# A decode kernel of two layers of cached attention and MLP on one core: w2 loaded by 14 rows a partition, wo in four transfers, softmax maxima and sums through TensorE, and a new order of the instructions

## The chip, the cores and the metric

The kernel runs on one core of a Trainium2 chip. The metric is the device time of one launch in microseconds (us). The engines are TensorE (PE, with its weight load PEld), VectorE (DVE), ScalarE (ACT), GpSimd (POOL) and SyncE (SP), which here only issues DMAs. Every engine works through its own list in order and waits on semaphores for the others.

## What is computed

Two equal layers: layernorm, attention over the last 1,024 positions of a cache of 4,096, residual; layernorm, MLP with silu, residual. Both layers use the same caches and the same weights. There are 8 rows (the batch, one new token each), D = 448, 16 query heads on 8 kv heads of 256, F = 1,792; all bf16.

```python
def attention(x):                       # x: 8 x 448
    q = (x @ wq) -> 16 heads of 256
    k = k_cache[:, :, 3072:4096, :]     # 8 rows x 8 kv heads x 1024 x 256; v likewise
    scores = q . k * 256 ** -0.5        # two query heads share a kv head
    o = softmax(scores) . v
    return o @ wo                       # 4096 x 448

def mlp(x):
    return silu(x @ w1) @ w2            # 448 x 1792, 1792 x 448

x = x + attention(layernorm(x)); x = x + mlp(layernorm(x))
x = x + attention(layernorm(x)); x = x + mlp(layernorm(x))
```

## The kernel before

**What is read.** The window of each row and kv head is one k and one v tile of 128 partitions x 2,048 elements (512 KB). The 128 tiles, 64 MB, are read once. They go through 30 slots of SBUF: the n-th load goes to slot n modulo 30 and waits until load n - 30 is used up. The order on SP's queue is: x, parts of wq and w1, the rest of wq (L444), the k tiles of row 0 (L500), then w2 in four transfers (L459), wo in one (L453), the v tiles of row 0, w1, the k tiles of row 1, its v tiles, and so on. w2 goes to 32 partitions with each transfer: partition 32j + p takes pairs of rows of the j-th quarter. wo goes to 128 partitions with one transfer. Both arrive in pieces of two rows, 1,792 bytes, since each pair of rows has places for the negative row means beside it. These means come from row sums: four groups of w2 and eight of wo, by turns on DVE (`tensor_reduce`, L479) and ACT (448 columns each with an accumulator, L487). Every row sum of wo waits for the whole of wo. The products with w2 (L762) and wo (L721) wait for the means.

**What is done with a tile, and in which order.** Both layers use a tile while it is in its slot. Layer 1 of row b + 1 and layer 2 of row b are woven together; between the layers of a row lies what the code calls its chain. Below, "0" or "1" behind a step's name is layer 1 or layer 2.

1. DVE transposes each k tile in place, in two halves (L636, 16 a row). PE forms the scores for four kv heads at a time (32 matmuls, L651), two lots for each layer, into a bank with head and position on the partitions.
2. Softmax: DVE takes the negative maximum of each partition (max, L663). Four partitions q hold the parts of one head, so DVE transposes (mT, L665), reduces over four (mg, L666) and transposes back (mb, L668). ACT takes the exponential (L671), PE permutes (perm, L673), DVE transposes 32 x 32 blocks (turn, L675). The sum of a head comes from a product with ones (l, L677), a reduction on DVE (lsum, L679) and a reciprocal (rl, L681).
3. PE multiplies with the v tiles, kv head by kv head (PV, 4 matmuls each, L687). ACT evicts the bank of 512 columns (oev, L694), PE transposes (oT, 4 matmuls, L696), and DVE evicts with the factor 1/l (oTev, L700). Layer 1 does this for heads 0 to 6 and then for head 7 alone, with a second eviction of the whole bank. PE multiplies with wo (32 matmuls, L721), ACT evicts (rowb, L727), and the fold (seven matmuls, L531 and L534) brings the row onto the partitions, added to x, with the mean in a column of its own.
4. The chain: DVE subtracts the mean and masks half columns (xb, L732). PE computes w1 (16 matmuls, L541), then the sum of squares (stat, four matmuls, L739). ACT scales it (var, L742), POOL takes the power -1/2 (L744). DVE transposes w1's result (w1T, L546), ACT takes tanh (L756), DVE finishes silu (hT, L757). PE multiplies with w2 (14 matmuls, L762) and folds; xb and stat follow again, x2b keeps the row on ACT (L768), then wq in two lots (L773), each with a transpose (qT, L778), a scaling by 1/sigma (qm, L779) on DVE, four matmuls (qx, L786) and an eviction on ACT (L790), which layer 2's scores wait for.
5. wo and the MLP of layer 2 are done for rows 0 to 6 together (`final_rows`, w1 and w2 through L541 and L856) while the last row's scores run, and for row 7 alone at the end (`final_last`).

The last chunk of 448 = 3 x 128 + 64 rows of w1 and wq lies in two halves of 64 partitions, one for either half of the columns. The mask sets the other half of the column vector to zero, and the matmuls read all 128 partitions.

**What sets the order.** The code does not write down a sequence. Each step is a task with an engine, keys that it reads and writes, and an estimated duration (`pe(...)`, `dve(...)`, `act(...)`, `pool(...)`, `dma(...)`). The class `Plan` gives each task a rank, the longest chain of estimated durations behind it. A list scheduler then gives each engine, when it comes free, the ready task of highest urgency, which is the rank plus an entry of the table `BIAS`, empty here. What comes out is fixed in the program: a list for each engine, with the semaphore waits. On the chip nothing is reordered.

Of the kernel before, what the change touches and what calls it, by code (L numbers as in the profile page):

```python
# [4 lines left out]
BF16 = mybir.dt.bfloat16  # L5
# [15 lines left out]
BIAS = {}  # L21
# [14 lines left out]
class Plan:  # L36
# [9 lines left out]
    def add(self, eng, fns, reads=(), writes=(), dur=0.1, row=-1, name="", dma_key=None, via="sp"):  # L46
        if not isinstance(fns, (list, tuple)):
            fns = [fns]
        t = Task(eng, list(fns), dur, row, name)
# [202 lines left out]
def bass_interleave_layers__sliding_block_cached__dense_activation_silu__decode_kernel(  # L252
# [43 lines left out]
    th = sb("th", [P, FC], F32)  # L296
    hT = sb("hT", [P, FC], BF16)
    q1s = sb("q1s", [P, NB, P], BF16)
    mm = [sb(f"mm{i}", [P, 32], F32) for i in range(2)]
    mg = [sb(f"mg{i}", [P, 8], F32) for i in range(2)]  # L300
    xb0 = sb("xb0", [P, XC + 1, NB], BF16)
    xl0 = sb("xl0", [P, NB], BF16)
    cols = sb("cols", [P, 10], BF16)
    fcols = sb("fcols", [P, 16], F32)
# [3 lines left out]
    e_sb = [qbd[i][:, 264:520] for i in range(2)]  # L308
    oT2 = [q1s[:, b, 0:2 * H] for b in range(NB)]
    x2b = [q1s[:, b, 32:32 + XC + 1] for b in range(NB)]  # L310
    oT1 = [q1s[:, b, 40:40 + 2 * H] for b in range(NB)]
    rl = [q1s[:, b, 72:72 + 2 * H].bitcast(F32) for b in range(NB)]
# [4 lines left out]
    eps4, nhalf, var4, rhalf = fcols[:, 9:10], fcols[:, 10:11], fcols[:, 11:12], fcols[:, 12:13]  # L317
    ones_b = ones_1.broadcast_to([P, P])
# [7 lines left out]
    C_O, C_ST = 128, 200  # L326
# [31 lines left out]
    SCRATCH = {R - 1: ["xrow", "xh", "sq8", "sqh8", "st8", "q1T", "sel", "sel_f", "nm8", "rh8"] +  # L358
# [10 lines left out]
    sel_f = SCR[:, 1152:1152 + 4 * H].bitcast(F32)  # L369
    big8 = SCR2[:, 0:512].bitcast(F32)  # L370
# [13 lines left out]
    const(cols[:, :], 0.0, ["cols0"])  # L384
    const(ones_1, 1.0, ["ones_1"], ["cols0"])
    for q in range(4):
# [3 lines left out]
    for i in range(2):  # L390
        const(mm[i][:], 0.0, [("mm", i)])
        const(mg[i][:], 0.0, [("mg", i)])
    const(qbd[0][:, 0:8], 0.0, [("pad", 0)])
    const(qbd[1][:], 0.0, [("pad", 1)] + QB(1, 0) + QB(1, 1), dur=0.2)
    for i in SC:
        const(bank[i][:], -1e30, bk(i), dur=0.6)
# [19 lines left out]
    for q in range(4):  # L416
# [6 lines left out]
    dve(lambda e: e.tensor_copy(sel_o[:], sel_f.rearrange("p (n a) -> p a n", a=2)), ["sel_f"], ["sel_o"], 0.1, -1,  # L423
        "init")
# [27 lines left out]
    def load_wo():  # L452
        dma(lambda e: e.dma_start(wo_sb[:].rearrange("p (h n) -> p h n", n=PW)[:, :, R0:M1],  # L453
                                  A_wo.rearrange("(h p a) n -> p h (a n)", p=P, a=2)), ["wo"], HD * D * 2, "wo",
            rate=375e3)

    def load_w2():
        for j in range(4):
# [290 lines left out]
    def up(b):  # L749
        w1_rows(XB, 1, lambda c: xbt[b][:, c:c + 1], b, [("xbt", b)], "w1")  # L750
# [274 lines left out]
```

## Time and profile before

| | us |
|---|---|
| runs without profile | 255.55, 252.28, 256.36 (median 255.55) |
| the profiled execution | 251.9 |
| its span, first to last instruction | 249.6 |
| PE busy (3,055 matmuls) | 165.3 |
| DVE busy (432) | 166.2 |
| ACT busy (151) | 60.1 |
| k transposes on DVE (L636), 128 | 83.3 |
| scores on PE (L651), 1,024 matmuls | 41.0 |
| products with v on PE (L687), 512 matmuls | 37.3 |
| maxima (L663), 16 of 0.424 | 6.8 |
| 77.3 MB on queue q1 | 82.6% of 16 DMA engines' span |

How to read it: in the profile's slices, each of 40 equal parts of the span has a digit, the busy share in tenths; `PEclk` is the clock that TensorE was granted, in tenths of full speed (mean 0.942 here), DMA the mean busy share of the 16 DMA engines, and GB/s what they moved. A chain of waits is followed back from the last instruction; each line gives start, length and what the time went to. "SPq" is SP's queue, where a DMA instruction waits until its slot is free. In a table by stages, each engine has its busy us and the number of its instructions in brackets.

### The profile page before, as it was taken

To read this page: it belongs to the slowest core of one execution; us is meant where nothing else is said; L and a number is where in the kernel's file an instruction comes from. 1 tells how busy PE (TensorE), PEld (TensorE's weight loads), DVE (VectorE), ACT (ScalarE), POOL (GpSimd) and SP (SyncE) were. 2 spreads that over 40 slices of the span, in tenths; PEclk is the share of its full clock that TensorE was granted. 3 is DMA by queue.
4 is the path that set the end of the run, shared out by engine and by line. 5 is a ranking of instruction groups with operands and counts; after the bars stand their busy time and mean duration, and the time that the engine had idled before them with its cause. 6 is when DMAs were issued, how large, how long until landed. Compare 5 with 4: busy or idle time off the path is not lost.

```text
span 249.6 us, 7017 instructions
## 1 busy us (share of the span) xinstructions
PE 165.3 (66%) x3055; PEld 85.2 (34%) x3055; DVE 166.2 (67%) x432; ACT 60.1 (24%) x151; POOL 23.0 (9%) x41
## 2 busy tenths in 40 slices
PE   0054211257687976878787787878788967888783
PEld 0053100012243334334334533443434434434532
DVE  6749536794885797599587768946783697534321
ACT  2000033721213221331331222232111331323221
POOL 1201000000000010100010010000000000001200
PEclk9999999999589999999997999999657999999995
DMA  6999999999999999999999899999967997300000
GB/s 173 416 407 351 200 278 387 409 413 418 407 362 301 412 410 362 389 412 403 315 411 409 322 376 413 410 343 412 407 257 259 418 392 294 158 3 4 3 1 3
DMA packets 22676, 78.13 MB, mean 313 GB/s; under 512 B 2279, under 2 KB 5366, under 8 KB 22262
## 3 DMA queue, kind: packets, MB, share of 16 engines
q1 hardware_dynamic: 22486, 77.31, 82.6%
q8 instruction: 24, 0.39, 0.6%
q10 hardware_dynamic: 160, 0.38, 0.5%
q14 instruction: 6, 0.05, 0.1%
HBM read 77.67 MB, written 0.01 MB: 311 GB/s over the span
## 4 chain that ended last, share of the span: by engine, by line
PE 34%; DMA 25%; DVE 21%; SPq 8%; ACT 5%; issue 4%; POOL 2%; DVEq 0%; ACTq 0%
DMA slot<-in_A_k_cache_dram 14%; DVE slot L636 11%; PE bank L651 11%; DMA wo_sb<-in_A_wo_dram 11%; PE bank L687 4%; DVE slot L479 3%; PE bank L773 3%; SPq L459 3%; SPq L500 3%; PE bank L541 3%; PE bank L721 3%; PE bank L786 2%; PE bank L762 2%; ACT qbd L790 2%; POOL fcols L744 2%
## 5 line engine op out<-in xcount | busy, mean ns | idle before, releaser
L636 DVE STREAM_TRANSPOSE slot<-slot 128x512 uint32<-128x512 uint32 x128 | 83.3, 686 | 15.3 <-DMA slot<-in_A_k_cache_dram 15.0
L651 PE MATMUL bank<-slot,qbd 128*16 128x256 bf16 (+1 forms) x1024 | 41.0, 305 | 15.1 <-ACT qbd L790 6.4
L687 PE MATMUL bank<-slot,qbd 128*8 128x512 bf16 (+7 forms) x512 | 37.3, 393 | 15.2 <-DMA slot<-in_A_v_cache_dram 9.2
L651 PEld LDWEIGHTS bank<-slot,qbd 128*16 128x16 bf16 (+1 forms) x1024 | 27.8, 94 | 23.5 <-ACT qbd L790 8.4
L687 PEld LDWEIGHTS bank<-slot,qbd 128*8 128x8 bf16 (+7 forms) x512 | 12.4, 89 | 29.7 <-DMA slot<-in_A_v_cache_dram 12.9
L773 PE MATMUL bank<-wq_sb,q1s 128*1 128x512 bf16 x256 | 19.9, 434 | 1.9 <-DVE q1s L732 1.9
L694 ACT ACTIVATE ot<-bank 128x512 bf16<-128x512 f32 x24 | 14.3, 597 | 26.6 <-PE bank L687 26.6
L721 PE MATMUL bank<-wo_sb,q1s 128*1 128x449 bf16 x288 | 19.1, 378 | 1.1 <-DVE q1s L700 1.1
L744 POOL TENSOR_TENSOR fcols<-fcols 128x1 f32<-128x1 f32 x17 | 9.4, 552 | 111.9 <-ACT fcols L742 111.9
L624 POOL TENSOR_TENSOR qbd<-q1s,fcols 128x256 bf16<-128x256 bf16 x16 | 9.8, 612 | 101.0 <-PE bank L673 54.2
L663 DVE TENSOR_REDUCE mm<-bank 128x1 f32<-128x256 f32 x16 | 6.8, 424 | 16.3 <-PE bank L651 16.3
L762 PE MATMUL bank<-w_sb,hT 128*1 128x449 bf16 x112 | 9.6, 434 | 9.2 <-DVE hT L757 9.2
L790 ACT ACTIVATE qbd<-bank 128x256 bf16<-128x256 f32 x16 | 6.0, 383 | 33.7 <-PE bank L708 19.6
L679 DVE TENSOR_REDUCE q1s<-bank 128x16 f32<-128x128 f32 x16 | 4.7, 291 | 13.7 <-PE bank L677 13.7
L479 DVE TENSOR_REDUCE slot<-wo_sb 128x6 f32<-128x2688 bf16 x4 | 11.5, 2945 | 3.3 <-DMA wo_sb<-in_A_wo_dram 3.3
L778 DVE STREAM_TRANSPOSE bank<-bank 128x512 f32<-128x512 f32 x16 | 11.4, 711 | 2.1 <-PE bank L773 2.1
L671 ACT ACTIVATE qbd<-bank,mm 128x256 bf16<-128x256 f32 x16 | 7.6, 472 | 18.2 <-DVE mm L668 9.5
L673 PE MATMUL bank<-qbd,perm 128*128 128x256 bf16 x16 | 4.6, 285 | 8.7 <-ACT qbd L671 8.7
L541 PE MATMUL bank<-w_sb,q1s 128*1 128x448 bf16 x144 | 8.6, 357 | 2.3 <-DVE q1s L732 1.8
L732 DVE SCALAR_TENSOR_TENSOR q1s<-bank,fcols 128x5 bf16<-128x5 f32 x17 | 3.7, 219 | 9.6 <-PE bank L534 9.6
L727 ACT ACTIVATE ot<-bank 128x450 bf16<-128x450 f32 x9 | 4.9, 546 | 18.3 <-PE bank L721 18.3
L596 PE MATMUL bank<-slot,wq_sb 128*128 128x16 bf16 x128 | 3.6, 174 | 8.4 <-DMA wq_sb<-in_A_wq_dram 8.4
(132 smaller groups left out, 181.9 us busy)
## 6 DMA issues: line engine op xcount, KB each, us to landing
slot<-in_A_k_cache_dram SPq DMA_DIRECT2D x64, 512.0 KB, 8.3
slot<-in_A_v_cache_dram SPq DMA_DIRECT2D x64, 512.0 KB, 10.5
wo_sb<-in_A_wo_dram SPq DMA_DIRECT2D x1, 3584.0 KB, 26.3
wq_sb<-in_A_wq_dram SPq DMA_DIRECT2D x3, 1024.0 KB, 9.1
w_sb<-in_B_w_dram SPq DMA_DIRECT2D x4, 392.0 KB, 18.8
w_sb<-in_B_w_dram SPq DMA_DIRECT2D x1, 1344.0 KB, 17.0
wq_sb<-in_A_wq_dram ACTq DMA_DIRECT2D x1, 256.0 KB, 3.5
wq_sb<-in_A_wq_dram SPq DMA_DIRECT2D x1, 256.0 KB, 4.1
```

What stands on the lines that cost most here:

```text
L479: dve(lambda e, rows=rows, s=s: e.tensor_reduce(s, rows[:, :, R0:M1].rearrange("p c (a n) -> p c a n", a=2), AX.X, ALU.add, negate=True), ...
L541: pe([lambda e, c=c, j=j: e.matmul(bank[bank_i][32 * j:32 * j + n, 0:D], lhs(c if c < 3 else 3 + j // 2), view(w1_sb[:], c * F + D * (j if ...
L636: dve(lambda e, v=v: e.transpose(v, v), [("slot", s)], [("slot", s)], 0.15 + n / 2 / 950, b, "KT%d" % k)
L651: fns.append(lambda e, w=w, j=j, kv=kv, cb=cb, par=par: e.matmul(sc[32 * j:32 * j + up_to, 0:256], w, kv, start=(cb == 0 and par == 0), st ...
L687: pe([lambda e, t=t: e.matmul(bank[OB[L]][32 * t:32 * t + m, :], pT_sb[L][:, 64 * t:64 * t + m], v[:, 512 * t:512 * t + 512], start=True, ...
L694: act(lambda e: e.activation(ot[:], bank[OB[L]][:], ACTF.Copy), bk(OB[L]), ["ot"], 0.62, b, "oev%d" % L)
L721: fns.append(lambda e, i=i, w=w, c0=c0: e.matmul(bank[XB][32 * (i % 4):32 * (i % 4) + 1, c0:c0 + D + 1], oT[:, oT_col(i):oT_col(i) + 1], w ...
L744: pool(lambda e: e.tensor_tensor(rhalf, var4, nhalf, ALU.pow), ["var4", "nhalf"], ["rhalf"], 0.54, b, "pow" + name)
L762: fns.append(lambda e, f=f, w=w, c0=c0: e.matmul(bank[XB][32 * (f % 4):32 * (f % 4) + 1, c0:c0 + D + 1], hT[:, f:f + 1], w, start=(f < 4), ...
L773: pe([lambda e, j=j, c=c, wb=wb, k2=k2: e.matmul(bank[wb][32 * j:32 * j + 1, :], xbt[b][:, xcol(c, k2):xcol(c, k2) + 1], view(wq_sb[:], c ...
L778: dve(lambda e, wb=wb: e.transpose(bank[wb][:], bank[wb][:]), bk(wb), bk(wb), 0.62, b, "qT%d" % k2)
L790: act(lambda e, qs=qs, k2=k2: e.activation(qbd[1][:, 8 + 256 * k2:264 + 256 * k2], qs, ACTF.Copy), bk(lb), QB(1, k2), 0.42, b, "qbd%d" % k2)
```

## The change

- **w2** comes in one transfer to 128 partitions; partition p takes rows 14p to 14p + 13, so w1's columns are read in steps of 14 to deliver hidden unit 14p + f at the right place.
- **wo** comes in four transfers of 896 KB, and each row sum waits for its own quarter.
- **Maxima:** DVE spreads a partition's maximum over four columns (mq, 128 x 4), an f32 matmul with a matrix `quad` brings the four parts of a head to each of its partitions (mx), and DVE takes the minimum over four columns (mb). mT, mg and the transposing mb are gone.
- **Sums:** the exponential on ACT accumulates each partition's sum; four f32 matmuls with `lsel` (l) add them by head, and DVE takes the reciprocal of one column (rl). lsum is gone. The factor 1/l is applied by ACT in oev, and ACT also does oTev.
- **Centred rows:** the fold adds the mean to all columns, so xb is a plain copy on ACT. The mask is gone from it; the last chunk of w1, wq and stat uses the 64 partitions that hold something. x is recovered at the end with a matmul by -1/128 where needed.
- **The last head of layer 1** goes into 256 columns (8 matmuls of 3 x 256) of the scores' bank, its eviction has 256 columns, and oT has two matmuls.
- **Row 7, layer 2:** P.V, oev, oT and wo go in two halves; silu takes tanh straight from the bank with the scale and two DVE operations.
- **Order:** a table `TIME` replaces the estimated durations and `BIAS` has some 290 entries. On PE, the sums and stat come earlier: in a steady row perm1, l0 and l1 stand before the last product of layer 1 and the first of layer 2, stat before w1; mx of layer 1 stands before the second lot of layer 2's scores. On DVE, maxima, turns and reciprocals of both layers stand together, ahead of the row's first k transpose. On ACT, both evictions of layer 1 come before rowb and xb, and oev of layer 2 behind them. SP's order is as before but for w2 (one issue) and wo (four). In the tail, w1 of rows 0 to 6 stands inside row 7's scores of layer 2, and their fold before row 7's products.

```diff
-BIAS = {}
+TIME = {"pe.S0.0": 0.0288, "pe.S0.1": 0.0288, "pe.S1.0": 0.0288, "pe.S1.1": 0.0288, "pe.PV0": 0.0538, "pe.PV1": 0.0538,
...
+BIAS = {"act.exp0": -98.9, "act.exp0@0": 5.6, "act.exp0@7": -50.9, "act.exp1": 113.3, "act.exp1@0": 56.6,
...
     def load_wo():
-        dma(lambda e: e.dma_start(wo_sb[:].rearrange("p (h n) -> p h n", n=PW)[:, :, R0:M1],
-                                  A_wo.rearrange("(h p a) n -> p h (a n)", p=P, a=2)), ["wo"], HD * D * 2, "wo",
+        for g in range(4):
+            dma(lambda e, g=g: e.dma_start(
+                wo_sb[:, 4 * g * PW:4 * (g + 1) * PW].rearrange("p (h n) -> p h n", n=PW)[:, :, R0:M1],
+                A_wo[1024 * g:1024 * (g + 1), :].rearrange("(h p a) n -> p h (a n)", p=P, a=2)), [("wo", g)],
+                HD * D // 2, "wo%d" % g, rate=375e3)
+
+    def load_w2():
+        dma(lambda e: e.dma_start(w2_sb[:].rearrange("p (g n) -> p g n", n=PW)[:, :, R0:M1],
+                                  B_w2.rearrange("(p g s) n -> p g (s n)", p=P, s=2)), ["w2"], F * D * 2, "w2",
             rate=375e3)
-
-    def load_w2():
-        for j in range(4):
-            dma(lambda e, j=j: e.dma_start(
-                w2_sb[32 * j:32 * j + 32, :].rearrange("p (g n) -> p g n", n=PW)[:, :, R0:M1],
-                B_w2[D * j:D * j + D, :].rearrange("(g p s) n -> p g (s n)", p=32, s=2)), [("w2", j)],
-                F * D // 2, "w2%d" % j, rate=375e3)
...
-                    loads, [("sums", key, g)], 0.48 * 2 * n, row, "rsum")
+                    load(i0), [("sums", key, g)], 0.48 * 2 * n, row, "rsum")
...
-        fns += [lambda e, a=a: e.matmul(bank[bank_i][:, col + XC * step:col + XC * step + nb],
-                                        row[:, a * (D + 1):a * (D + 1) + 1].broadcast_to([P, P]), rhs_a[a], start=False,
-                                        stop=True, skip_group_check=True) for a in range(2)]
+        fns += [lambda e, a=a: e.matmul(view(bank[bank_i][:], col, [(step, XC + 1), (1, nb)]),
+                                        row[:, a * (D + 1):a * (D + 1) + 1].broadcast_to([P, P]),
+                                        rhs_a[a].unsqueeze(1).broadcast_to([P, XC + 1, nb]), start=False, stop=True,
+                                        skip_group_check=True) for a in range(2)]
...
-            bank[bank_i][32 * j:32 * j + n, 0:D], lhs(c if c < 3 else 3 + j // 2),
-            view(w1_sb[:], c * F + D * (j if c < 3 else j % 2), [(64, 7), (1, 2), (2, 32)]),
-            start=(c == 0), stop=(c == KC - 1), tile_position=(0, 32 * j), skip_group_check=True)
+            bank[bank_i][32 * j:32 * j + n, 0:D], lhs(c, j // 2),
+            view(w1_sb[half(c, j // 2), :], c * F + D * (j if c < 3 else j % 2), [(1, FC), (FC, 32)]),
+            start=(c == 0), stop=(c == KC - 1), tile_position=(half(c, j // 2).start, 32 * j), skip_group_check=True)
...
-        dve(lambda e: e.transpose(m[:], m[:]), [("mm", L)], [("mm", L)], 0.21, b, "mT%d" % L)
-        dve(lambda e: e.tensor_reduce(mg[L][:, 0:4], m[:, 0:16].rearrange("p (n q) -> p n q", q=4), AX.X,
-                                      ALU.min), [("mm", L)], [("mg", L)], 0.17, b, "mg%d" % L)
-        dve(lambda e: e.transpose(m[:].rearrange("p (n q) -> p n q", q=4),
-                                  mg[L][:].unsqueeze(2).broadcast_to([P, 8, 4])),
-            [("mg", L), ("mm", L)], [("mm", L)], 0.21, b, "mb%d" % L)
-        act(lambda e: e.activation(e_sb[L], x, ACTF.Exp, bias=m[:, 0:1], scale=1.0),
...
+        dve(lambda e: e.tensor_scalar(mq, sel4, mneg, None, op0=ALU.mult), [K[0], "sel4"], [K[4]], 0.13, b, "mq%d" % L)
+        pe(lambda e: e.matmul(mx, quad[:], mq, start=True, stop=True, skip_group_check=True), [K[4], "quad"], bk(LB[L]),
+           0.2, b, "mx%d" % L)
+        dve(lambda e: e.tensor_reduce(bias, mx, AX.X, ALU.min), bk(LB[L]), [K[1]], 0.15, b, "mb%d" % L)
+        act(lambda e: e.activation(e_sb[L], x, ACTF.Exp, bias=bias, scale=1.0, accum_out=acc),
+            bk(SC[L]) + [K[1]], EK[L] + [K[2]], 0.6, b, "exp%d" % L)
...
-        pe(lambda e: e.matmul(lb[:, 0:128], ones_b, view(pT_sb[L], 0, [(64, 4), (1, 32)]), start=True, stop=True),
-           PT[L] + ["ones_1"], bk(LB[L]), 0.1, b, "l%d" % L)
-        dve(lambda e: e.tensor_reduce(rls, lb[:, 0:128].rearrange("p (t n a) -> p n t a", t=4, a=2), AX.XY, ALU.add),
-            bk(LB[L]), [("rl", b, L)], 0.27, b, "lsum%d" % L)
-        dve(lambda e: e.reciprocal(rls, rls), [("rl", b, L)], [("rl", b, L)], 0.22, b, "rl%d" % L)
+        pe([lambda e, t=t: e.matmul(lr[32 * t:32 * t + 32, :], lsel[:], acc, start=True, stop=True,
+                                    tile_position=(0, 32 * t), skip_group_check=True) for t in range(4)],
+           [K[2], "lsel"], bk(LB[L]), 0.05, b, "l%d" % L)
+        dve(lambda e: e.reciprocal(rlr, lr), bk(LB[L]), [K[3]], 0.15, b, "rl%d" % L)
...
+        act(lambda e: e.activation(o_t, src[1], ACTF.Copy, scale=sm[b][:, 4 * L + 3:4 * L + 4]),
+            bk(src[0]) + [("sm", b, L, 3)], okey, 0.62, b, "oev" + name)
...
+        act(lambda e: e.activation(dst.rearrange("p (a n) -> p a n", a=2)[:, :, c0:c1], o_c, ACTF.Copy),
+            bk(LB[L]), keys, 0.2, b, "oTev" + name)
...
-        dve(lambda e: e.scalar_tensor_tensor(
-            out=xbt[b], in0=bank[YB][:, 0:XC * XS:XS], scalar=bank[YB][:, XC * XS:XC * XS + 1], in1=mask5,
-            op0=ALU.add, op1=ALU.mult), bk(YB) + M5, [("xbt", b)], 0.17, b, "xb" + name)
+        act(lambda e: e.activation(xbt[b], bank[YB][:, 0:XC * XS:XS], ACTF.Copy), bk(YB), [("xbt", b)], 0.2, b,
+            "xb" + name)
```

Lines of the kernel after that the prediction and the result name: SP's tile loads are L596, w2 L557, wo L551, row sums L575 and L583, k transposes L736, scores L751, max L766, mq L767, mx L768, mb L770, exp L771, perm L773, turn L775, l L777, rl L780, PV L786 and (last head) L794, oev L802, oT L806, oTev L810, wo L831, rowb L837, xb L842, stat L848, w1 L641, hT L867, w2 L872, qm L889, qx L896.

## The prediction

> **What bounds the kernel now.** I read three views in this order: the page's slices, the chain that ended last, and timelines where the chain says that something is late. The slices come first:
>
> ```profile
> DVE  6749536794885797599587768946783697534321
> PEclk9999999999589999999997999999657999999995
> DMA  6999999999999999999999899999967997300000
> GB/s 173 416 407 351 200 278 387 409 413 418 407 362 301 412 410 362 389 412 403 315 411 409 322 376 413 410 343 412 407 257 259 418 392 294 158 3 4 3 1 3
> ```
>
> The DMA engines are busy in nearly every slice until about 216 us, and then idle: one stream of 64 + 64 loads of 512 KB, then a tail of compute alone, 249.6 - 216.2 = 33.4 us. The best slices move 410 to 418 GB/s. Slices five and six (25 to 37 us) move half of that with the engines just as busy. By stages of 5 us (after the busy times: clock, DMA share, GB/s):
>
> ```profile
> 15.00:20.00 5.00, 3.77 (x130) 3.62 (x130) 3.90 (x6) 0.00 (x0) 0.00 (x0) 1.00 1.02 410
> 25.00:30.00 5.00, 0.51 (x12) 0.01 (x4) 3.28 (x6) 0.00 (x0) 0.00 (x0) 1.00 1.06 200
> 30.00:35.00 5.00, 1.88 (x32) 0.94 (x32) 0.16 (x1) 0.00 (x0) 0.00 (x0) 1.00 1.07 210
> 35.00:40.00 5.00, 0.17 (x1) 0.10 (x1) 4.64 (x6) 4.57 (x15) 0.00 (x0) 1.00 1.05 380
> ```
>
> The slow stage is w2: its four transfers land at 28.98, 31.00, 32.98 and 35.13 us, 2.0 us for 0.4 MB each. wo, which goes to all 128 partitions in pieces as long (1,792 bytes), follows at 380. Next the chain:
>
> ```profile
> 18.71 26.33 DMA wo_sb<-in_A_wo_dram
> 45.10 2.83 issue
> 47.93 8.66 DVE slot L479 x3
> 57.10 3.13 PE bank L721 x18
> ...
> 99.03 7.37 DMA slot<-in_A_k_cache_dram
> 106.41 1.31 DVE slot L636 x2
> 107.89 0.96 PE bank L541 x14
> ```
>
> The start hangs on wo's landing at 45.04 us, then on four row sums by DVE (11.5 us in all), which the first row's wo matmuls wait for. Later each row's chain runs through compute (Q.K, softmax, P.V, wo, w1, w2, wq) and touches DMA once: the last k load of the next row, here landing at 106.4. So rows are limited nearly equally by compute and by the stream. A gapless row of the stream is 16 loads x 1.28 us = 20.5 us; each row's hT (L757) ends 24.4, 21.8, 21.3, 22.9, 22.3, 25.8 and 21.6 us after the one before it (rows 1 to 7). In the first, fourth and sixth of these the clock is low for a time; the others take 21.3 to 22.3. SyncE's waits say why the stream has holes:
>
> ```profile
> SPq L500 <- PE bank L651: 71.7, 7, 13.9
> SPq L500 <- PE bank L687: 20.1, 19, 2.5
> ```
>
> Loads wait for slots, which the second layer's scores (L651) and products (L687) give back. A load issued 3.9 us or more before the previous one lands leaves no hole; one issued 2.0 to 2.5 us before leaves 0.8 to 1.9. Over all rows some 9 us of holes come so.
>
> **The change, part by part.** The sum is made on the profiled execution, 251.9 us with a span of 249.6.
>
> *w2 as one transfer to 128 partitions.* From 23.0 to 34.7 us, 2.41 MB move in 11.7 us. At wo's 380 GB/s they take 6.3: **-5.4 us** for everything behind it in the queue. Bounds: 4.9 (at wo's mean of 370 with a start of 0.3) to 5.9 (at the k loads' 410). The issue of w2 on SP shrinks from 8.48 us (four of 2.1) to about one of 2.2, with three more issues for wo at most 2.2 each. SP is far ahead of the stream there, so that is free; were it not, 6.3 of saved issue would be a further gain.
>
> [...]
>
> *wo in four transfers.* Each row sum then waits for its own quarter. Today DVE starts at 45.06 and ends at 56.59, after the last v load (55.24). After: wo lands at 39.6, its first quarter at about 32; four sums of 2.95 with softmax in between end by 47, and the last v load lands at 55.24 - 5.4 = 49.8. So the sums leave the path, and the v loads take their place: oev, turn, 28 and 4 wo matmuls end near 53.4 instead of 60.2. Behind that point the first row has holes and a low clock. At the next row's hT (88.81) I take **7.1 us** earlier in all, 1.7 beyond w2's part. Bounds 6.3 (the stream stays just ahead: 5.4 and half of the 1.9 us hole at the last load of row 1) and 8.35 (with the whole hole and a warm PE).
>
> *Steady rows.* I follow the path in segments; row 2 before, then after:
> - w1's end to hT: 1.76, then 1.49. The four statistics matmuls (0.25) come before w1 (0.96), so variance (0.26) and power (0.56) run beside it; w1's turn (0.67), tanh (0.27) and hT (0.17) remain with their handovers.
> - hT to the last query scaling (L779): 5.27, then 5.3. As many k transposes stand in front of it on DVE as before.
> - to the end of the second layer's scores: 4.91, then 5.15. One maxima matmul (mx) now stands before them on PE.
> - to the first product: 1.0, then 1.2. The second mx and its multiply stand before the turn. Gone from DVE are two 32-column transposes and a small reduce (0.19 + 0.17 + 0.21); added are a multiply and a reduce of 4 columns (about 0.16 each, by the small DVE rows).
> - to the eviction (oev): 1.74, then 2.4. The second permutation (0.285) and the sums' matmuls stand before the last products, and oev now waits for the reciprocal (1/l is its scale), with the second turn (0.44) in front of it on DVE.
> - to wo's end: 3.60, then 3.45. The last head's eviction has 256 columns (0.38, as L790, not 0.60), and oTev on ACT is not behind a 0.69 us k transpose.
> - to w1's end: 3.06, then 2.75. The centring (L732) today waits behind two k transposes (106.41 to 107.72); on ACT it follows rowb.
>
> Sum 21.34, then 21.74. Before's rows 1, 2 and 4 take 21.80 on average, since some wait for k. For five rows I take **-0.3**. Bounds: -2 (every row at 21.3) and +3 (the f32 matmuls dearer, below). DVE loses some 2.3 us of 17.8 a row, and ACT gains as much of its 7; neither bounds a row, so this buys only the places named above. What ACT takes over queues there: oev of the second layer stands behind rowb and xb, and tanh behind oTev, 0.16 to 0.2 us each, for which PE has other products to do.
>
> *The f32 matmuls* (mx, four for l) have no row in before. From below: the one-column bf16 row L739, 0.167 us each and 0.25 for four in a stream. [...]
>
> *The tail,* from row 7's first maximum: f32 matmuls ahead of products +0.45; reciprocal before oev +0.25; the rows' w1 (16 matmuls, 1.01) inside row 7's scores, partly in idle time, +0.7; h8 and the fold of rows 0 to 6 ahead of softmax and products +0.6. Against it statistics first -0.3, product and wo in halves -0.5, one eviction less before tanh with a product in its place -0.4. That is +0.8; with six more handovers of some 0.06, **+1.2** (bounds -0.5 to +2).
>
> Sum: -7.1 - 0.3 + 1.2 = -6.2, so 245.7 us in an execution like the profiled one. The runs shown are 251.9, 252.28, 255.55 and 256.36, by my reading with the clock's low stretches lying differently. Since their mean is 2.1 above the profiled run, I add 0.8 and say **246.5**.
>
> **The rivals.**
>
> *The stream sets the rows.* If the slots come free 3.9 us ahead throughout, holes vanish and rows fall to about 20.9 (20.5, and 0.4 for single loads that land up to 1.2 us late today, some 6 us in all, though SP was ahead). For it: DVE and the later PE steps have slack, and scores that free slots come as early as before. Against it: the segments above. Five rows less 0.9: 251.9 - 7.1 - 4.5 + 1.2 = 241.5.
>
> *The start's gain, partly eaten.* Every row 0.8 longer than before, from mx, the sums' matmuls and the reciprocal ahead of oev at the top of my bounds: 251.9 - 7.1 + 5 x 0.8 + 2 = 250.8, with the median's 0.8 251.6.
>
> [...]
>
> *Half-row matmuls.* w1, wq and statistics now use 64 rows in their last chunk. If each change of shape emptied the array, at 0.285 (an isolated matmul, L673) five times a row, it would be 7 x 1.4 = 10 us: 255.7. Against it, the fold today mixes 128- and 64-row pieces, and its five take 0.39 us, 0.07 each as in a uniform stream. [...]
>
> *w2 no faster.* If the half rate came from the pieces and not from the partitions: -1.7 and no more at the start: 251.1. wo's 380 speaks against it.
>
> **How the numbers follow.** My forecast (243.5 to 249.5) gets 0.42, the stream 0.22, the eaten gain 0.19, f32 0.07, half rows 0.06, w2 no faster 0.04. The range takes in the first three, 0.83: 239 to 254. A measurement can tell about 2%: against the median of 255.55, faster is under 250.4 and slower over 260.7. The first two cases are faster, 0.64; eaten, w2 and most of half rows are the same, 0.27; f32 and the rest 0.09.
>
> **What would show it.** Right: no stage at 200 GB/s, w2 in 4 to 5 us, wo landed by 40; L575 spread between quarters, done before the last v load; rows of 21.3 to 22; mx at 0.2 to 0.3; SP waits of L596 as before. Wrong: oev waiting long for DVE, DVE waiting for mx, scores later, or more low-clock stretches; or rows of 20.9, with SP never late.

## The result and the profile after

The kernel after takes 274.62 us (median of four runs, 273.21 to 285.9) against 253.92 for the kernel before (252.15 to 256.36): a ratio of 1.0825, with a 95% interval of 1.0704 to 1.0946. It is slower by 8%. The forecast was 246.5 us, in a range of 239 to 254, and faster. The profiled execution of after is 275.65 us, its span 273.8 (before: 251.9 and 249.6). The ratios compare only the quicker executions of each kernel, those within 1.5% of its fastest.

The page's slices come first:

```profile
PE   0052333768888979888979798888879888999874
PEclk9999999975999599979997997999799989999997
DMA  7999999999399849977994999399949984000000
GB/s 191 407 416 390 381 396 410 420 406 397 132 364 410 356 168 363 412 295 244 408 408 174 372 412 407 114 351 413 385 124 382 409 327 156 2 2 0 2 3 0
```

The two slices at half rate are gone: the fifth and sixth now show 381 and 396 GB/s, where before had 200 and 278. But behind the start the stream has a hole in every row (132, 168, 244, 174, 114, 124), and PE is busier than before: 202.4 us against 165.3. The table by stages of 5 us answers to the one shown of before:

```profile
20.00:25.00 5.00, 1.94 (x60) 1.66 (x57) 4.09 (x6) 0.00 (x0) 0.00 (x0) 1.00 1.03 396
25.00:30.00 5.00, 0.00 (x0) 0.00 (x0) 4.90 (x9) 0.60 (x1) 1.19 (x2) 1.00 1.05 380
30.00:35.00 5.00, 3.08 (x60) 1.99 (x64) 4.93 (x6) 3.60 (x12) 0.00 (x0) 1.00 1.06 381
```

w2 takes 4.2 us from the last k tile's landing to its own (27.04 to 31.25), before 8.1 (27.05 to 35.13). wo lands at 40.76, the last v tile of row 0 at 50.96, w1 at 54.22, each 4.3 us earlier than before. In this execution the stream also began late: the last of the three large wq loads landed at 16.74 us, in before at 14.67. The eight k tiles behind it made up for this, since they came 1.3 us apart throughout, in before the last three 1.7 to 2.4. So the start gained what the forecast said, less this delay. The chain, from the third row on, says where the time went:

```profile
135.84 0.29 PE bank L848 x4
136.13 3.46 PE bank L641 x13
139.62 0.67 DVE bank L646
140.28 0.36 DVE slot L736
```

The second line is w1. In the chain of before it is 0.96 us (L541); here 3.46, and it is on the chain in every row and at both ends of the tail. The costliest groups confirm it; first before, then after:

```profile
L541 PE MATMUL bank<-w_sb,q1s 128*1 128x448 bf16 x144 | 8.6, 357 | 2.3 <-DVE q1s L732 1.8
```

```profile
L641 PE MATMUL bank<-w_sb,q1s 128*1 128x448 bf16 x108 | 23.5, 984 | 0.0
L641 PE MATMUL bank<-w_sb,q1s 64*1 64x448 bf16 x36 | 8.7, 957 | 0.0
L768 PE MATMUL bank<-q1s,quad 128*128 128x4 f32 x32 | 6.2, 263 | 8.7 <-DVE q1s L767 5.1 <-ACT qbd L900 3.6
L777 PE MATMUL bank<-q1s,lsel 128*32 128x1 f32 x128 | 3.9, 182 | 6.3 <-DVE wo_sb L578 4.6 <-DVE q1s L780 0.9 <-DVE qbd L775 0.7
```

One w1 matmul lasts 984 ns instead of 357, alike with 128 and with 64 rows (957). Sixteen of them take 3.5 us instead of 0.96. There are ten such groups in the kernel: seven rows' chains and row 7's, the group for rows 0 to 6, and the last row's: 10 x 2.5 = 25 us. The f32 matmuls are small: each mx is recorded as two of about 0.26 us that overlap, and the four of a sum as eight of 0.18.

### The profile page after: what moved, and what is told of

It reads as the page before. It is cut to its first block, busy times and chain, and to the rows that moved or that the text cites. A ratio compares the mean times of both kernels' runs of the same rounds, so it can differ in the third digit from the quotient of the medians.

```text
span 273.8 us, 7340 instructions
## 1 busy us (share of the span) xinstructions
PE 202.4 (74%) x3232; PEld 88.5 (32%) x3232; DVE 157.5 (58%) x363; ACT 68.5 (25%) x209; POOL 23.1 (8%) x41
## 4 chain that ended last, share of the span: by engine, by line
PE 60%; DVE 13%; SPq 12%; ACT 6%; DMA 5%; issue 3%; POOL 0%; ACTq 0%; DVEq 0%
PE bank L751 13%; PE bank L641 13%; PE bank L786 9%; SPq L551 6%; PE bank L831 6%; PE bank L883 5%; DMA slot<-in_A_v_cache_dram 5%; SPq L596 4%; DVE slot L736 4%; ACT ot L802 2%; PE bank L896 2%; PE bank L627 2%; PE bank L768 2%; ACT qbd L900 2%; DVE bank L646 2%
## 5 line engine op out<-in xcount | busy, mean ns | idle before, releaser
L736 DVE STREAM_TRANSPOSE slot<-slot 128x512 uint32<-128x512 uint32 x128 | 84.2, 690 | 12.2 <-DMA slot<-in_A_k_cache_dram 11.0
L751 PE MATMUL bank<-slot,qbd 128*16 128x256 bf16 (+1 forms) x1024 | 41.0, 304 | 11.3 <-DVE slot L736 7.6
L786 PE MATMUL bank<-slot,qbd 128*32 128x512 bf16 (+7 forms) x480 | 35.5, 393 | 1.5 <-DMA slot<-in_A_v_cache_dram 1.0
L646 DVE STREAM_TRANSPOSE bank<-bank 128x448 f32<-128x448 f32 x10 | 6.7, 666 | 50.9 <-PE bank L641 50.9
L641 PE MATMUL bank<-w_sb,q1s 128*1 128x448 bf16 (+1 forms) x144 | 31.6, 977 | 0.0
L751 PEld LDWEIGHTS bank<-slot,qbd 128*16 128x16 bf16 (+1 forms) x1024 | 23.9, 91 | 23.4 <-DVE slot L736 13.1
L883 PE MATMUL bank<-wq_sb,q1s 128*1 128x512 bf16 (+1 forms) x256 | 23.8, 475 | 0.3 <-ACT q1s L842 0.3
L831 PE MATMUL bank<-wo_sb,q1s 128*1 128x449 bf16 x288 | 17.9, 374 | 0.0
L802 ACT ACTIVATE ot<-bank,q1s 128x512 bf16<-128x512 f32 x17 | 11.7, 687 | 21.3 <-PE bank L786 11.7
L872 PE MATMUL bank<-w_sb,q1s 128*1 128x449 bf16 x112 | 9.6, 425 | 8.7 <-DVE q1s L867 8.7
L786 PEld LDWEIGHTS bank<-slot,qbd 128*32 128x32 bf16 (+7 forms) x480 | 11.3, 91 | 11.0 <-DMA slot<-in_A_v_cache_dram 2.8
L775 DVE STREAM_TRANSPOSE qbd<-bank 128x256 bf16<-128x256 bf16 x16 | 7.5, 468 | 11.9 <-PE bank L773 11.9
L768 PE MATMUL bank<-q1s,quad 128*128 128x4 f32 x32 | 6.2, 263 | 8.7 <-DVE q1s L767 5.1
L771 ACT ACTIVATE qbd<-bank,q1s 128x256 bf16<-128x256 f32 x16 | 7.6, 473 | 18.6 <-DVE q1s L770 18.6
L810 ACT ACTIVATE q1s<-bank 128x28 bf16<-128x28 f32 (+3 forms) x25 | 4.7, 187 | 28.7 <-PE bank L806 28.7
L575 DVE TENSOR_REDUCE slot<-wo_sb 128x6 f32<-128x2688 bf16 x4 | 11.8, 2943 | 0.0
L766 DVE TENSOR_REDUCE q1s<-bank 128x1 f32<-128x256 f32 x16 | 6.8, 425 | 8.4 <-PE bank L751 8.4
```

The source lines that it names most:

```text
L575: dve(lambda e, rows=rows, s=s: e.tensor_reduce(s, rows[:, :, R0:M1].rearrange("p c (a n) -> p c a n", a=2), AX.X, ALU.add, negate=True), ...
L641: pe([lambda e, c=c, j=j: e.matmul(bank[bank_i][32 * j:32 * j + n, 0:D], lhs(c, j // 2), view(w1_sb[half(c, j // 2), :], c * F + D * (j if ...
L646: dve(lambda e: e.transpose(bank[bank_i][:, 0:D], bank[bank_i][:, 0:D]), bk(bank_i), bk(bank_i), 0.56, row, name + "T")
L736: dve(lambda e, v=v: e.transpose(v, v), [("slot", s)], [("slot", s)], 0.15 + n / 2 / 950, b, "KT%d" % k)
L751: fns.append(lambda e, w=w, j=j, kv=kv, cb=cb, par=par: e.matmul(sc[32 * j:32 * j + up_to, 0:256], w, kv, start=(cb == 0 and par == 0), st ...
L768: pe(lambda e: e.matmul(mx, quad[:], mq, start=True, stop=True, skip_group_check=True), [K[4], "quad"], bk(LB[L]), 0.2, b, "mx%d" % L)
```

## The experiments

Four kernels went to one chip first, to tell the step of 14 in w1's columns from the 64-row halves and from the new order. The diffs of this section show of long lines the part that changes.

**The step taken out of the kernel after.** w2's layout is changed so that a partition has seven pairs of rows 256 apart; w1's columns are then read in steps of 2 as in before (the last lines of the diff are the load of w1's last 64 rows).

```diff
-B_w2.rearrange("(p g s) n -> p g (s n)", p=P, s=2)
+B_w2.rearrange("(g p s) n -> p g (s n)", p=P, s=2)
...
-view(w1_sb[half(c, j // 2), :], c * F + D * (j if c < 3 else j % 2), [(1, FC), (FC, 32)])
+view(w1_sb[half(c, j // 2), :], c * F + 64 * (j if c < 3 else j % 2), [(256 if c < 3 else 128, 7), (1, 2), (2, 32)])
...
-src[3 * P:D, h * m:(h + 1) * m]
+src[3 * P:D, :].rearrange("p (g a c) -> a p g c", a=2, c=P)[h]
```

> The kernel after, but w2's 14 rows of a partition are seven pairs 256 rows apart (still one transfer to 128 partitions in pieces of 1,792 bytes), so that w1's columns are read in steps of 2 elements again; w1's last 64 rows are loaded in pieces of 128 columns for this. The order on every engine is that of after. Theory (the step of 14): the 16 matmuls of w1 fall from 3.5 us to about 1.0, ten times in the kernel: 274.6 - 25 = 249.6, and perhaps 2 to 4 less since the clock is low less often. Rival (64-row halves and changes of shape make w1 slow): w1 stays at 3.4 and the time within 2 us of 274.6. Rival (the new order and its waits carry the loss): w1 falls, but PE waits as long elsewhere, time above 260.

Measured: 247.75 us, ratio 0.9805 (0.9722 to 0.9888). w1's 16 matmuls take 1.03 us (the second number of the line, PE's busy time for them in a stretch of 6 us):

```profile
126.00:132.00 6.00, 1.03 (x16) 0.28 (x16) 0.85 1.03 410
```

Expected was 249.6, or 2 to 4 less. The theory of the step holds, the rivals fall: 64-row halves are still in this kernel, and so is the order.

**The same layout as after in the kernel before**, with `load_w2` as in after and nothing else:

```diff
-view(w1_sb[:], c * F + D * (j if c < 3 else j % 2), [(64, 7), (1, 2), (2, 32)])
+view(w1_sb[:], c * F + D * (j if c < 3 else j % 2), [(1, FC), (FC, 32)])
```

> The kernel before with w2 by 14 rows a partition alone (one transfer, w1's columns in steps of 14); 128-row matmuls with the mask, and the order of before. Theory (the step): w1 3.4 to 3.5 us instead of 0.96, ten times, less 5.4 at the start: 253.9 + 25 - 5.4 = 273. Rival (64-row halves): w1 stays at 0.96, 248.5. Both expect w2 to land in 4 to 5 us.

Measured: 267.69 us, ratio 1.0659 (1.0551 to 1.0767), against 273 expected. Of the 5 us that are missing, 2 lie in the kernel before, which took 251.95 beside it and not 253.92; the rest isn't explained. This one part carries most of the loss by itself, with 128-row matmuls and the old order. w1 takes 3.40 us:

```profile
L539 PE MATMUL bank<-w_sb,q1s 128*1 128x448 bf16 x144 | 30.6, 982 | 1.3 <-DVE q1s L730 1.1
```

**The kernel after with w2 as before**:

```diff
-B_w2.rearrange("(p g s) n -> p g (s n)", p=P, s=2)
+B_w2[D * j:D * j + D, :].rearrange("(g p s) n -> p g (s n)", p=32, s=2)
...
-view(w1_sb[half(c, j // 2), :], c * F + D * (j if c < 3 else j % 2), [(1, FC), (FC, 32)])
+view(w1_sb[half(c, j // 2), :], c * F + D * (j if c < 3 else j % 2), [(64, 7), (1, 2), (2, 32)])
```

> The kernel after with w2 in its four old transfers to 32 partitions and w1's columns in steps of 2; all the rest and the order as after. Theory (the step): w1 back to about 1.0; the start loses the 5.4 us of w2, so 5 us above the run with pairs, about 255. Rival (64-row halves): w1 3.4 and 280. If the other edits are worth the 1.7 at the start and nothing else, it ends near 252 to 254.

Measured: 254.34 us (248.59 to 260.41) against 251.95 (247.17 to 258.19), near the 255 expected, without a clear verdict. w1 takes 1.05 us, and w2's parts land 2.0 us apart again (29.13, 31.13, 33.23, 35.09). So no gain is shown of all that is in the change besides w2.

**The step by itself.** The kernel before, with another step in each row:

```diff
+STEP = {b: [(1, k), (k, D // k)] for b, k in ((0, 1), (1, 4), (2, 7), (3, 8), (4, 14), (5, 16), (6, 32), (6.5, 28), (7, 64))}
...
-view(w1_sb[:], c * F + D * (j if c < 3 else j % 2), [(64, 7), (1, 2), (2, 32)])
+view(w1_sb[:], c * F + D * (j if c < 3 else j % 2), STEP[row])
```

> The kernel before, with w1's columns read with another step in each row: 1, 4, 7, 8, 14, 16, 32 and 64 elements for rows 0 to 7, 28 for rows 0 to 6 in the tail (hidden units then meet other rows of w2, so the output differs). Theory (a moving read costs by how far apart its elements lie): the 16 matmuls take 0.96 at steps 1 and 2 and 3.4 at 14, and grow with the step between. If the four column tiles only lose their overlap, the time stops at about 3.5 whatever the step beyond 14; if each step to another memory word costs, 32 and 64 are dearer than 14. Rival (64-row halves): 0.96 at every step.

One execution, 265.98 us. Stages cut so that each holds one row's 16 matmuls; the first number behind the length is PE's busy time for them, then the weight loads, the clock, DMA. The rows 1 to 6, steps 4, 7, 8, 14, 16 and 32:

```profile
85.00:91.00 6.00, 1.75 (x16) 0.33 (x16) 1.00 1.02 408
107.00:113.00 6.00, 2.92 (x16) 0.33 (x16) 1.00 1.02 411
131.00:138.00 7.00, 3.31 (x16) 0.33 (x16) 1.00 1.03 411
156.00:162.00 6.00, 3.40 (x16) 0.34 (x16) 1.00 1.03 410
179.00:185.00 6.00, 3.39 (x16) 0.33 (x16) 1.00 1.01 404
203.00:210.00 7.00, 3.43 (x16) 0.33 (x16) 1.00 1.02 411
```

The cost grows with the step up to 8 elements, 16 bytes, and then stands still (28, in the tail's group for rows 0 to 6, 3.23); 64 elements, in row 7, add some again: 4.05. So take words of 16 bytes, the step at which the time stops growing, and count those that a read comes through: at step 8 or more one per element, 448 in a matmul, 16 x 448 = 7,168, in 3.31 to 3.43 us, 0.46 to 0.48 ns each. At step 7 it is 7/8 of that, 6,272 words, in 2.92 us, 0.47 ns each. At step 4 half, 3,584, in 1.75 us, 0.49 each. At step 2 a quarter, 1,792 words, would be 0.84 us, under the 0.93 to 0.96 measured, below which no step went. So in these runs a word costs, not an element. Two elements to a word (step 4) take 1.75 us, 1.8 times the 0.96 of four (step 2).

The expectation had set 32 dearer than 14 as the sign of words, and a stop at 3.5 as the sign that the four column tiles merely lose their overlap. The time did stop, but that sign was ill chosen: from 8 elements on every element has a word of its own, so words stop there too. Against lost overlap speak the steps of 4 and 7, which follow the count of words, and that the time does not rise when TensorE's clock falls (3.49 and 3.50 us, last section).

**Words or jumps, and who reads.**

```diff
+J4 = [(c, j) for j in range(4) for c in range(KC)]
+STEP = {0: TWO, 1: SEV, 2: TWO, 3: [(2, 7), (14, 32), (1, 2)], 4: [(4, 7), (28, 16), (1, 4)], 5: SEV,
+        6: [(8, 7), (56, 8), (1, 8)], 6.5: TWO, 7: [(28, 16), (1, 28)]}
+ORDER = {b: J4 if b < 2 else C4 for b in STEP}
```

> The kernel before with other reads of w1's columns by row (hidden units then meet other rows of w2, so the output differs). From the steps run (16 matmuls: step 4 1.75 us, 7 2.92, 8 3.31, 14 3.40, 32 3.43): a theory of words, a new 16-byte word of the moving operand costs a slot, neighbours in the same word ride along. Then row 3 (two neighbours at each step of 14) takes half of 3.4, 1.7; row 4 (four neighbours at each step of 28) and row 6 (eight at 56) fall to the floor of about 1.0; row 7 (28 neighbours) too. A theory of long steps (any jump of 28 bytes or more costs) gives 1.7 for row 3, 0.9 to 1.0 for row 4 as well, but for row 7 no more than row 6: it would part from words only at step 8 against 14, equal above. Rows 0 and 1 run the 16 matmuls one column tile after the other (steps 2 and 14), so that no two of them run side by side: if the four tiles share one reader, step 14 stays near 3.4 to 3.6 in that order too; if each tile has its own, slow one, it rises towards 4 x 3.4. Rows 2 and 5 repeat steps 2 and 14 as they were.

One execution, 256.14 us. Rows 1, 2, 3, 4 and 5 (one tile after the other at step 14; step 2; two neighbours at 14; four at 28; step 14):

```profile
86.00:92.00 6.00, 3.45 (x16) 0.45 (x16) 1.00 1.03 412
111.00:117.00 6.00, 0.97 (x16) 0.29 (x16) 1.00 1.02 408
134.00:140.00 6.00, 1.79 (x16) 0.34 (x16) 1.00 1.03 416
157.00:163.00 6.00, 0.94 (x16) 0.29 (x16) 1.00 1.02 410
179.00:185.00 6.00, 3.40 (x16) 0.34 (x16) 1.00 1.03 412
```

Neighbours in a word ride along: two halve the time (1.79), four bring it to the floor (0.94), and eight or 28 (rows 6 and 7) take 0.93. The length of the jump to the next word does not count between 8 and 32 elements (3.31 to 3.43 us in the run before). The order of the tiles changes nothing (3.45 and 3.40), so the four do not each have a slow reader of their own; they share the pace of 0.47 to 0.48 ns a word. Row 0 (1.70, step 2 tile by tile; 1.66 at step 1 in the run before) can't be read: in the first row, other matmuls take about double too (w2's 14 take 1.66 us, later 0.92).

**Is the rest of the change worth anything?** Three more kernels with the pairs, on one chip with the run just told: the kernel before with the pairs alone, the kernel after with the pairs and `BIAS = {}`, and the kernel before with the pairs, wo's four transfers and each row sum behind its own quarter. The pairs are the layout of the first experiment; the last of the three has besides wo's four transfers, as in after, and:

```diff
-    row_sums(wo_sb, "wo", ["wo"],
+    row_sums(wo_sb, "wo", lambda i: [("wo", i // 4)],
```

> The kernel before with w2 in one transfer to 128 partitions by seven pairs of rows, w1's columns in steps of 2, and nothing else; the order as before. Theory: the start gains 5.4 us and the rows nothing, 252 - 5.4 = 246.5, ratio about 0.979, so as fast as the kernel after with the same pairs (247.8, ratio 0.98): the other edits are worth nothing together. Rival: the other edits carry part of that ratio, and this one stays at 0.985 to 1.0, since the row sums of wo (11.5 us on DVE after the last quarter) still hold the start.

> The kernel after with the pairs, and with an empty BIAS table: the planner's own order from the same durations. If the table's order is worth something, this is slower than the run with pairs (ratio 0.98) by 0.3 us or more a row, 250 to 253 and a ratio of 0.99 to 1.0. If the order is worth nothing, ratio 0.98. If the table costs (rows of 22.05 us against 21.3 to 21.8 before), rows fall to 21.5 and the ratio to 0.965.

> The kernel before with the pairs and with wo in four transfers, each row sum behind its own quarter; softmax, centred rows and last head as before (the planner moves 4 wo matmuls and 8 scores a row by itself). Theory: the row sums leave the path of the first row, 1 to 2 us below the run with pairs alone, ratio about 0.973. Rival: the first row waits for the v loads anyway, ratio as with pairs alone.

The kernel before with the pairs alone: 246.67 us, ratio 0.9892 (0.9777 to 1.0007). The time is the expected 246.5, but the ratio lies in the rival's range of 0.985 to 1.0, and its interval takes in both. With wo in four transfers besides: 243.9, 0.9801 (0.9702 to 0.99), where the theory said 0.973; since the interval takes in that and the 0.9892 as well, what wo's four transfers are worth is not shown. The kernel after with the pairs and an empty table: 252.8, 1.0168 (1.0071 to 1.0265), slower than the 0.99 to 1.0 expected. So the table's order is worth 2.6 to 3.6% to this kernel (0.9805 above, and 0.991 below, with the table), each ratio taken to the kernel before on its own chip. The row segments hint where: its rows at full clock are shorter without the table (21.62 against 22.05 us), but its first row is longer, 26.5 against 25.1 and 25.5 in the two profiles with the table, the end 28.5 against 26.3 and 25.6, and rows 4 and 5 lose 2.4 to 2.9 us each while the clock is low.

The last four ran on a third chip, beside each other. The first of them has the maxima through TensorE in the kernel before with pairs and wo's four transfers (to make room, tanh's result and hT move into `q1s`):

```diff
-        dve(lambda e: e.transpose(m[:], m[:]), [("mm", L)], [("mm", L)], 0.21, b, "mT%d" % L)
...
+        dve(lambda e: e.tensor_scalar(mg[L][:, 0:4], sel4, m[:, 0:1], None, op0=ALU.mult), [("mm", L), "sel4"],
+            [("mg", L)], 0.13, b, "mq%d" % L)
+        pe(lambda e: e.matmul(mx, quad[:], mg[L][:, 0:4], start=True, stop=True, skip_group_check=True),
+           [("mg", L), "quad"], bk(LB[L]), 0.2, b, "mx%d" % L)
+        dve(lambda e: e.tensor_reduce(m[:, 0:1], mx, AX.X, ALU.min), bk(LB[L]), [("mm", L)], 0.15, b, "mb%d" % L)
```

> The kernel before with the pairs, wo in four transfers, and the maxima through TensorE (mq, f32 matmul, reduce of four columns) instead of two transposes and a reduce; sums, centred rows and last head as before. Theory: the maxima through TensorE are a longer chain (in the kernel after, max to the start of the exponential takes 1.43 to 1.46 us, before 1.16), so rows of layer 1 and 2 are 0.2 to 0.3 longer each time it ends last: 2 to 4 us over the kernel without it, ratio about 0.99 to 0.995 against 0.98. Rival: DVE's 0.45 us less a softmax is worth as much, ratio 0.98; or worth more, 0.97.

Measured: 242.61 us, ratio 0.9725 (0.967 to 0.9779). It is the fastest of all, and my theory was wrong by its sign. On this chip the kernel without the maxima through TensorE has 0.987 (0.9819 to 0.9921, below), so it gains 1.5%; against the 0.9801 (0.9702 to 0.99) of that kernel's earlier run the intervals overlap. The chain from max to the exponential did get longer (1.46 us against 1.16 in layer 1, 3.1 to 3.4 against 1.42 in layer 2), and its rows at full clock are no shorter (21.4 to 22.7 us). What differs is the granted clock: its mean was 0.99 or more in five of six executions and 0.976 in one, against 0.930 to 0.979 in the kernel without the maxima through TensorE. That the clock makes the difference is not shown: that kernel took 240.84 us at 0.968 and 245.83 at 0.978. The page's row of clocks shows no low stretch but the last:

```profile
PEclk9999999999999999999999999999999999999996
```

The planner also moved other steps in this kernel (in a steady row layer 2's sum now stands behind w1 and stat and no longer ahead of them, and no products stand between wo's matmuls), so the maxima and the order are not told apart. Why the clock stays up, and whether another kernel would share it, these runs don't say.

The next two repeat kernels told above, side by side:

> The kernel after with the pairs once more, on one chip with the next. Theory: all edits but w2 and wo are worth nothing together, so the two agree within 1%, at ratios of 0.98. Rival: they are worth something, and this one is faster by over 1%.

> The kernel before with the pairs and wo in four transfers once more, beside the one above. Theory: ratio 0.98 and within 1% of it. Rival: over 1% slower than it.

Measured: after with the pairs 247.73 us, 0.991 (0.9861 to 0.9959); before with pairs and wo 245.9, 0.987 (0.9819 to 0.9921). They agree within 1%, as expected, though at 0.99 and not at 0.98. So beside w2's transfer and wo's four parts the change brings nothing: maxima, softmax sums, centred rows on ACT, the last head in 256 columns and the halves come to nothing together, in this order. Since the maxima alone, in the order above, gave 0.9725 on the same chip, the others or the order cost about as much as the maxima gained.

The last one, the kernel after with the pairs, drops the table's entries for rows 1 to 6 (70 of 296).

> The kernel after with the pairs, and with the BIAS entries only for row 0, row 7 and single steps; rows 1 to 6 in the planner's own order. In the run with an empty table, rows at full clock took 21.62 us (22.05 with the table), but the first row 26.5 and the end 28.5 (25.1 and 26.3 with it). Theory: the table earns its gain at both ends and gives 0.4 a row back in between; then this kernel has six rows of 21.65, 2.5 us below the run with pairs, ratio about 0.97. Rival: the ends come from the whole order, or low-clock stretches eat it: ratio 0.98 or above.

Measured: ratio 0.9836 (0.9735 to 0.9937), which rests on two of six executions; the six took 243.55 to 255.69 us, with a median of 253.06. Inconclusive, and no sign of the theory's 0.97: no row of the profiled execution is under 22.1 us, and the clock is low in five stretches of its rows 1 to 6.

## Why the prediction was wrong

**The step that failed** is in "Steady rows": "to w1's end: 3.06, then 2.75". It takes w1 at 0.96 as before, and nowhere prices the read in steps of 14, though the front of this document names it. No rival has it either. Measured in after, the segment is 5.33 to 5.35 us, and 2.85 to 2.88 with steps of 2. The missing term is 10 x 2.5 = 25 us: ten groups of 3.5 us instead of 0.96 to 1.03. No row of before reads w1 in steps of 14, so its profile held no price. What lay at hand was the step itself. I had looked at the new access on the DMA's side alone, where it is good (w2 in 4.2 us instead of 8.1), and not at the engine that reads what the DMA has laid down.

After less the run with pairs (the profile of its second run, span 246.9), from the end of hT in row 0: 273.8 - 246.9 = 26.9 us, of which 4.0 until that point, 17.9 in the seven rows behind, and 5.0 from there to the end. 2.5 + 7 x 2.5 + 2 x 2.5 = 25 is w1 itself, and 1.5 of the first part is the stream's late start in this execution (row 0's last v tile at 50.96 against 49.41). In rows 1 to 6 of after the clock falls to 0.5 for 3.4 us (6.8 in row 1), 1 to 4 us behind w1's end, about where wq runs: 6.6 to 6.8 us from hT to the first query scaling, against 5.55 at full clock. This stretch is worth 1.1 a row. The run with pairs has low stretches too, in three of its seven rows (23.3, 25.5 and 27.0 us), so that they nearly cancel in the difference. In the kernel before with the step of 14 the clock is low behind w1 in rows 0 to 2 only, so I can't call it a consequence of w1.

**The other steps, by the runs without the step:**

- w2 and wo: 5.4 was forecast, 4.3 measured in after, whose stream began 2.1 us late. In the eight other profiles of kernels with w2 in one transfer whose large wq loads landed within 0.5 us of before's, the last v tile of row 0 lands at 49.1 to 49.5 us, 5.8 to 6.1 before the 55.24 of before; three more profiles with w2 in four transfers have 54.3 to 54.7. So the term was right, at about 5 to 6. w2 went from 8.1 us to 4.2 and wo from 9.9 to 9.5. The issue of wo in four parts took SP 16.2 us instead of the 8.8 I allowed; it was hidden, since SP was still ahead of the stream (the last of these issues ended at 30.0 us, wo landed at 40.76).
- wo's row sums: they end at 48.5 (forecast 47), and the last wo matmul of row 0 at 54.9 (forecast 53.4, before 60.2). Right in kind; 1.2 of the 1.5 us is the later landing of the v tiles (50.96, forecast 49.8). But the 7.1 us at the next row's hT did not come: hT of row 1 is 5.0 to 5.9 us earlier in six profiles of kernels with the pairs, and 3.3 and 3.8 in the two with the table shortened or empty. The 1.7 beyond w2's part is missing. The hole in the stream behind row 0's loads did not shrink, it grew, from 1.9 us to 3.1 in the kernel before with pairs and wo's four transfers and to 2.7 with the maxima besides. And the first row's matmuls stayed at about half pace: w2's 14 take 1.66 us in row 0 of all these profiles, 0.92 in later rows at full clock.
- Steady rows: the segments of the run with pairs, at full clock, against those forecast (in brackets), in us: w1 to hT 1.35 (1.49), to the query scaling 5.56 (5.3; it is the first of the two lots, which is the one on the chain, though the prediction calls it the last), to the end of the scores 5.33 (5.15), to the first product 1.27 (1.2), to oev 2.33 (2.4), to wo's end 3.30 (3.45), to w1's end 2.85 (2.75). The sum is 22.0, the forecast 21.74. At full clock the method held to 0.3 us a row; what broke the forecast is a price that it did not contain. The chain of that run, row 2 to 3, shows the terms in place (waits of up to 0.08 us are not shown):

```profile
114.51 0.36 PE bank L770 x2
114.86 1.01 PE bank L753 x32
115.90 0.44 DVE q1s L768
116.36 0.24 DVE q1s L769
116.65 0.39 PE bank L770 x2
117.11 1.48 PE bank L788 x24
...
118.84 0.47 DVE qbd L777
119.32 0.04 DVE q1s L782
119.44 0.69 ACT ot L804
```

  These are mx (L770), the scores that it delays, max and mq, mx again, the products, the second turn, the reciprocal and oev, in the order and with the waits of the forecast.
- DVE loses 1.1 us a row (busy 166.2 to 157.5 us over eight rows) and ACT gains as much (60.1 to 68.5), half of the 2.3 in the prediction, which hung no term of the sum on it.
- "A load issued 3.9 us or more before the previous one lands leaves no hole" reads the profile of before too strictly: loads issued 5.5, 6.1 and 6.8 us ahead left 1.1 to 1.3 us. They are among the late single loads that the rival on the stream counts apart.
- f32 matmuls: mx takes 0.36 to 0.39 with its two records, forecast 0.2 to 0.3. The 0.07 that the forecast gives to f32 among its slower cases did not come true. The terms counted for them, 0.45 in the tail and the upper bound of 3 us over five rows, were the author's estimates, and no run shows them; the runs show these 0.36 to 0.39 for each mx, and 5.33 us instead of the forecast 5.15 for the segment to the end of the scores.
- Half rows: w1 1.03 against 0.93 to 0.96, wq 1.17 against 1.09, so 0.25 us a row for three groups, not 1.4. The rival fell, with a small price that I had put at nothing.
- The tail, here from row 7's hT to the end: 25.6 us against 25.2, so +0.4, forecast +1.2. In after itself it is 30.6, from two slow groups of w1.
- "w2 no faster" and "the stream sets the rows" fell: 380 GB/s, and rows of 22.0 without waiting for k.
- The sum: without the step the time, 247.7 us, is near the forecast 246.5, but that is in part luck. The kernel before took 252 us beside these runs and not 255.55; the gain is 1 to 2% where the forecast, 246.5 to 255.55, had 3.5%. The start was counted 1 to 2 us too high and the rows 0.3 too short each, the tail 0.8 too long.

## What to carry to other kernels

A new layout has two users: price what the DMA gains and also what each engine then pays to read it, in the innermost steps of its access. For the moving operand of a matmul, count the 16-byte words that are visited; here each cost 0.46 to 0.49 ns at steps of 4 to 32, so that steps up to 2 bf16 elements were free (0.93 to 0.97 us for 16 matmuls) and those of 8 to 32 took 3.4 to 3.6 times as long as the 0.96 of step 2. Both can be had: pairs of rows 256 apart kept the full-width transfer and the step of 2, and turned a loss of 8% into a gain of 1 to 2%.

## What was not expected of the hardware

- The slow read does not follow TensorE's clock. In row 0 of after, with a granted clock of 0.50 for 2.1 us of it, and in a row at full clock, 16 matmuls take the same, 3.49 and 3.50 us. w2's 14 matmuls do follow it: in after 0.92 us at full clock (row 3), 1.66 at a granted clock of 0.50 (row 1). The two lines of w1 in after:

```profile
56.00:62.00 6.00, 3.49 (x16) 0.30 (x16) 0.66 1.03 407
136.00:142.00 6.00, 3.50 (x16) 0.31 (x16) 1.00 1.02 410
```

- A step of 64 elements costs more than one of 32 (4.05 against 3.43 us); these runs don't show why.
- A change that lengthened the softmax chain made the kernel faster by 1.5% beside the one without it, and five of its six executions had a mean clock of 0.99. The cause is open.
- The granted clock in the records does not tell all: in row 0 of several profiles, that kernel's among them, it reads 1.00, yet w2's 14 matmuls take 1.66 us, as they do where it reads 0.50.
